# Two attention and mixer layers on one core: the second layer's channel mixers in groups of 3, 4, 3, 3, 3 tiles, a third buffer for VectorE's softmax blocks, and new ranks and instruction orders

## The chip, the cores and the metric

The kernel runs as one program on one core of a Trainium2 chip. The metric is the device time of one execution in microseconds. Before the change it is 1023.24 us, the median of three runs (1022.93 to 1025.7).

## The reference, cut to what matters

A sequence of 2048 rows of 448 numbers goes through attention, mixer, attention, mixer, with the same weights in both rounds:

```python
def _A_ref(x, wqkv, wo):                      # 16 heads of 28
    q, k, v = ...                             # from x @ wqkv
    scores = jnp.einsum("bhqd,bhkd->bhqk", q, k) * (Dh ** -0.5)
    p = _softmax(scores, axis=-1)
    o = jnp.einsum("bhqk,bhkd->bhqd", p, v)
    return ... @ wo
def _B_ref(x, w1, w2, w3, w4):
    h = _gelu(_layernorm(x) @ w1)
    hs = shifted_by_rows(h) @ w2              # four column groups, shifted by 1, -1, 2, -2 rows
    x1 = x + hs
    return x1 + _gelu(_layernorm(x1) @ w3) @ w4
x = x + _A_ref(_layernorm(x), A_wqkv, A_wo)
x = x + _B_ref(_layernorm(x), B_w1, B_w2, B_w3, B_w4)
# and both once more
```

Scores are 2048 x 2048 for each of 16 heads and two rounds; each of them needs an exponential.

## The kernel before, in words

**Tiles.** The rows are 16 tiles of 128. Attention works on blocks: 128 keys by 512 queries (or twice 128 by 256) of one head, one bank of the matmul accumulator (PSUM). There are 2048 blocks. Four heads form a head group, and a segment is one chunk of queries (`CHUNKS`: 4, 4, 4, 2, 2 tiles) with one head group and a run of key tiles (`ORDER`).

**Who takes the exponential.** `t_scores` lets TensorE write scores (line 1650) into banks 0 to 2 and banks 3 and 4 in turn; each such set is a *unit* of three or of two blocks, and `t_exp` lets ScalarE take the exponential of a whole unit in one instruction (line 1888), into PT, which has 15 places, six units deep. ScalarE takes each unit in order and is reserved for this from the first to the last. Some blocks go to VectorE instead, either from bank 6 or 7 or from bank 2 of a unit, which then has only two blocks for ScalarE (a *ring* block). Such a block is five VectorE instructions: `d_first` (line 1732) scales the scores out of PSUM into an integer buffer y, and `d_chain` (lines 1759, 1761, 1763 and 1766) makes 2 to that power with a cubic polynomial in a float buffer `fb` and adds the exponent. Before, y is `yd[0]` or `yd[1]`; `fb` has three buffers (`FB`), used also by the tanh form of GELU (`tanh_gelu`, lines 2152 to 2155) and by the softmax division (line 1995 and the transfer before it). For short times at the beginning and in the second layer, spare places of `vaug` serve too. A block is given to VectorE only if a y and a PD buffer are free at that moment in the plan, if VectorE's planned load is under `DTH` or `DDTH`, and if the rates `R_RATE` (ring) and `D_RATE` (the others) for that stretch allow it.

**PV and the division.** `t_pv` (line 1046) sums probabilities times V in bank 5, `t_norm` copies the sum out (lines 1969, 1971), spills it if the segment is not the last of its row, or divides by the row sums; `t_outproj` then applies wo.

**The mixer.** `t_mixA` multiplies by w1 (chunk by chunk), `t_mixB` does w2, w3 and GELU for a group of tiles from `BGROUPS`, and `t_w4` the last product. A group's w3 product comes in 14 parts of 128 features; a part of a group of n tiles is 128 n columns wide, and two parts share one bank when n is 2. While exponentials are still to come, VectorE copies each part out of PSUM (line 2313) and ScalarE takes one GELU over all 14 (line 2335), with a table load before it and one before the next exponential. After the last exponential (the plan's event "tail") ScalarE takes the GELU of each part straight from PSUM (line 2309). The groups before are tiles 0-2, 3-6, 7-10, 11-12 and 13-15 in both layers. `TANHW` marks one group of layer one that takes its GELU with tanh.

**What sets the order.** A planner (`Sched`) runs all these tasks in a simulated time with assumed costs. The dictionary `RANK` gives each task its priority; `Q_LEAD`, `K_FIRST`, `W_POS` and others say when loads and projections start. While TensorE would rest, the planner inserts fillers, four small matmuls on the identity matrix (lines 588 and 2381). The list of operations is then edited: `MOVES` puts single operations behind others of their engine, and `WEAVE`, a string with one letter for each operation (t TensorE, s ScalarE, v VectorE, g GpSimd, d the transfer queue), gives the order in which the engines' lists are merged. `rearranged` refuses an order in which an operation would read other data. Within an engine the instructions run in the order written.

Of the kernel before, what the change touches and what calls it, by code (L numbers as in the profile page):

```python
# [68 lines left out]
    "ttttvgssvvttttttttvvvvvvtvvvtvtstgtstsvtttvvtvvtvvtsttvvtsvvtttstvttstvttvvtgtsvtttvvstvttsvttvtttsvtttvttsttv",  # L69
    "svtgvgvvtttstvtttttvtttstvttvttvtdttttsvtvttvttsvttvtdttvtttvttvdstttttvstttttdvtstvtdtttttvtttttstvdttttvvstt",  # L70
    "vtsvttttttvvtvgtdtgttsvvtttttttvtsvtgttgvtttttsvttdttgttvttdttsvtdttvttdtvtdstvtdvttttsvtgtttttttvtstttttgttts",
    "vttttdvstttvtgsvtttvtttttttvtdsvttdtttdtsttvttdtgtsttvttttttstvttttttgtvtstvtdtttstvttttttttgttsttttttsttvtvtg",
    "tsttvttvtttvstvttvttttvttstttvtsvdtttdtvtvdvvsdvtvtttdttttvtsdvttvtdttdtvtsvtvdtttvtvtsttttvtttvttttstttttttts",
    "vtttvtttvstdttttvtgtttstvttttttsvtttttvstttvtttvttttsttvttttttsvtvttvtvtvvtsttvtvststtvdtttttgtttdvtstttttttvs",
    "tttttttttdtgsvtttttttsvgttttdtgdvsttdtvtgstvttttttttttsttttttsttvtttgtsttvttttttstvttgttttvstttvttdtsdttvttttt",
    "ttvsttttvtttsttvttvtvtvvtvstttvvsvtvttvtttttttvsttttvttsttvtttvttstvttdttdvsttttttttvtgttsttttstttttttttttsttt",
    "vtttvstgttvddsvtdtvttvdttttsvttttvtvttvvvsvtttvtvvsvtvttvtvttvttvttvsttttvttsvttgttttvtdtsdvttttdvsttvtttttttt",
    "tvttsvttdvttvvtvtdvsvttvdttvtttttdttttvsttsttvsttttttvttsttttvttvtttsvttttvtttsttttttvttttttttvtsttttvtttstvtt",
    "vttttttttvtsttttvtttvsttttvdtvsttttttvttttsttvttttttgtsttttttvtsttvtttvttdttttvstttttvtttsvtttdtvtttdtsvtttttt",
    "tttvtttstttvttvtttttsvtttttvsttttttvttttttttvsttvtttttvsgtttdtttvsttttvttttttsttvtttttvtgstttttvtstvttttttttvt",  # L80
# [691 lines left out]
RLO = 5  # L772
RHI = 7
RPRIO = 1
DWIN = 2
DTH = 0.4
XSHUT = (8, 83)
DLO = 6
DHI = 13
DPK = 2  # L780
DDTH = 1.3
# [6 lines left out]
TANHW = {(0, 0): 0, (0, 3): 0, (0, 7): 0, (0, 11): 1, (0, 13): 0, (1, 0): 0, (1, 3): 0, (1, 7): 0, (1, 11): 0, (1, 13): 0}  # L788
Sched.AGED = 0
Sched.TARGET = 0.695  # L790
Sched.LOW = 0
Sched.WIN = 1.582
Sched.LWIN = 3.6
GSL = 0
# [1691 lines left out]
```

## Time and profile before

| what | value |
|---|---|
| median of three runs | 1023.24 us |
| the profiled execution's own time | 1025.44 us |
| its span, first to last instruction | 1023.6 us |
| the first exponential of a unit starts at | 15.15 us |
| ScalarE's first table load for the GELU of the tail at | 969.87 us |
| operations in the plan (TensorE, ScalarE, VectorE, GpSimd, queue) | 7914, 880, 1572, 458, 362 |
| of them units of exponentials, blocks on VectorE, fillers | 782, 110, 837 |

An operation of the plan on TensorE is up to four matmuls; the profile counts them one by one. 110 blocks on VectorE appear in the profile as 109 in `yd` and one in `vaug`. Three stages follow from the table: a start of 15 us, a stage of exponentials of 955 us, and a tail of 54 us.

In profile rows, "x" is a count, "busy" the union of the group's time, "mean ns" the mean duration of one. An arrow "<-" names the output and its input, or, after a duration of idleness, what ended it.

### The profile page before, as it was taken

The numbers are of one execution on the slowest core, as the hardware profiler recorded it, in microseconds if no ns is written. First come the engines' busy times: TensorE is split into PE (matmuls) and PEld (weight loads), VectorE is DVE, ScalarE is ACT, GpSimd is POOL, SyncE is SP. The second block draws the span as 40 slices with busy tenths as digits, with TensorE's granted clock in tenths as the row PEclk, the third lists the DMA queues.
The fourth block names the chain that finished last, engine by engine and source line by source line (L and its number), as shares of the span: only waits on it lengthen the run. The fifth ranks groups of instructions, "written<-read, shape, count | busy, mean of one in ns | idle before, by whom it ended". The sixth has DMA issues, their size and how long they took to land.

```text
span 1023.6 us, 35818 instructions
## 1 busy us (share of the span) xinstructions
PE 968.4 (95%) x16107; PEld 408.1 (40%) x16109; DVE 814.0 (80%) x1572; ACT 981.7 (96%) x894; POOL 293.5 (29%) x462
## 2 busy tenths in 40 slices
PE   8999999999999999999999999999999999999998
PEld 4332443443333254343433443443433433444565
DVE  8777999989888958876877868698798589866651
ACT  8999999999999999999999999999999999999942
POOL 3312021531453016252325112012624120532230
PEclk9999999999999999999999999999999999999999
DMA  4634412320321014022231114423302020121101
GB/s 126 161 103 128 116 45 79 53 39 23 76 61 28 12 37 97 22 48 33 52 106 38 33 55 149 139 65 101 64 25 38 17 68 13 34 56 32 26 12 34
DMA packets 99393, 62.55 MB, mean 61 GB/s; under 512 B 68712, under 2 KB 88552, under 8 KB 99240
## 3 DMA queue, kind: packets, MB, share of 16 engines
q1 hardware_dynamic: 99240, 60.27, 23.2%
q8 instruction: 126, 2.06, 0.9%
q14 instruction: 27, 0.22, 0.1%
HBM read 28.16 MB, written 16.76 MB: 44 GB/s over the span
## 4 chain that ended last, share of the span: by engine, by line
ACT 70%; PE 24%; DVE 3%; DMA 1%; issue 1%; SPq 0%; DVEq 0%
ACT PT L1888 64%; PE ps L1055 14%; PE ps L1650 5%; PE ps L1046 4%; ACT h2T L2335 2%; PE ps L2381 1%; ACT fb L2154 1%; ACT L1888 1%; ACT hT L2136 0%; DMA rT<-ub 0%; DVE h2T L2313 0%; ACT L2335 0%; DMA obf<-in_A_x_dram 0%; DMA rscr<-rT 0%; DVE PD L1766 0%
## 5 line engine op out<-in xcount | busy, mean ns | idle before, releaser
L1888 ACT ACTIVATE PT<-ps 128x1024 bf16<-128x1024 f32 (+1 forms) x782 | 887.2, 1328 | 3.7 <-PE ps L1650 2.9
L1650 PE MATMUL ps<-qT,kT 32*128 32x512 bf16 (+1 forms) x2304 | 269.9, 335 | 24.1 <-ACT PT L1888 18.1
L1046 PE MATMUL ps<-PT,vaug 128*32 128x512 bf16 (+1 forms) x2420 | 246.2, 341 | 0.7 <-ACT PT L1888 0.2
L1055 PE MATMUL ps<-xT,w 128*32 128x512 bf16 (+4 forms) x2656 | 178.1, 344 | 5.0 <-DVE h2T L2313 3.4
L1650 PEld LDWEIGHTS ps<-qT,kT 32*128 32x128 bf16 x2304 | 69.7, 91 | 256.0 <-ACT PT L1888 224.7
L2381 PE MATMUL ps<-ident 128*32 128x256 bf16 x3348 | 145.1, 276 | 2.4 <-POOL ident L1140 1.5
L1046 PEld LDWEIGHTS ps<-PT,vaug 128*32 128x32 bf16 x2420 | 74.1, 95 | 89.4 <-issue 71.0
L2381 PEld LDWEIGHTS ps<-ident 128*32 128x32 bf16 x3348 | 94.3, 97 | 28.9 <-issue 11.8
L1995 POOL TENSOR_TENSOR otn<-ub,fb 128x512 bf16<-128x512 f32 (+1 forms) x31 | 35.8, 1154 | 212.8 <-DMA fb<-rscr 212.8
L1732 DVE TENSOR_SCALAR yd<-ps 128x512 int32<-128x512 f32 x109 | 74.5, 685 | 22.8 <-PE ps L1650 21.4
L1055 PEld LDWEIGHTS ps<-xT,w 128*32 128x32 bf16 (+1 forms) x2656 | 69.5, 95 | 56.8 <-issue 23.3
L1761 DVE SCALAR_TENSOR_TENSOR fb<-fb,yd 128x512 f32<-128x512 f32 x109 | 79.7, 734 | 0.7
L1055 PE MATMUL ps<-w,h2T 128*32 128x448 bf16 x1120 | 75.4, 355 | 4.4 <-ACT h2T L2335 4.3
L1759 DVE SCALAR_TENSOR_TENSOR fb<-yd 128x512 f32<-128x512 uint16 x109 | 78.3, 722 | 0.8
L1766 DVE SCALAR_TENSOR_TENSOR PD<-yd,PD 128x512 int16<-128x512 int16 x109 | 75.9, 698 | 1.6
L2313 DVE CAST h2T<-ps 128x512 bf16<-128x512 f32 (+1 forms) x70 | 44.4, 634 | 16.0 <-PE ps L1055 14.9
L1388 POOL TENSOR_TENSOR sq<-qT 128x512 bf16<-128x512 bf16 x24 | 28.5, 1190 | 96.1 <-DVE qT L1447 93.3
L1388 POOL TENSOR_TENSOR sq<-kT 128x512 bf16<-128x512 bf16 (+2 forms) x32 | 30.4, 950 | 83.1 <-DVE kT L1402 80.0
L1763 DVE TENSOR_SCALAR PD<-fb 128x512 bf16<-128x512 f32 x109 | 50.9, 468 | 1.0
L1055 PE MATMUL ps<-xT,wk_pad 128*32 128x512 bf16 (+2 forms) x576 | 47.6, 359 | 0.8 <-DVE kT L1402 0.3
L1055 PE MATMUL ps<-xT,wq_pad 128*32 128x512 bf16 x512 | 43.2, 382 | 0.5 <-issue 0.5
L1650 PE MATMUL ps<-wk_pad,kT 32*128 32x512 bf16 x256 | 39.6, 384 | 4.3 <-ACT PT L1888 3.8
(189 smaller groups left out, 1195.4 us busy)
## 6 DMA issues: line engine op xcount, KB each, us to landing
uscr<-ub SPq DMA_DIRECT2D x28, 256.0 KB
ub<-uscr SPq DMA_DIRECT2D x28, 256.0 KB, 7.0
fb<-rscr SPq DMA_DIRECT2D x24, 256.0 KB
xnd<-xn SPq DMA_DIRECT2D x28, 128.0 KB, 2.3
xd<-x_res SPq DMA_DIRECT2D x16, 224.0 KB, 2.1
x_res<-xd SPq DMA_DIRECT2D x16, 224.0 KB, 4.5
w<-in_B_w_dram SPq DMA_DIRECT2D x5, 448.0 KB, 5.4
obf<-in_A_x_dram SPq DMA_DIRECT2D x16, 112.0 KB
```

The source lines that it names most:

```text
L1046: return lambda e: e.matmul(out=out, lhsT=lhsT, rhs=rhs, start=start, stop=stop, **kw)
L1055: r.append(e.matmul(out=out[c:c + w, :], lhsT=lhsT[:, c:c + w], rhs=rhs, start=start, stop=stop, tile_position=(0, c)))
L1388: return both("sq", 0.15 + NW * 0.0018, 0.07 + NW * 0.00104, lambda e: e.tensor_tensor(out=sq[:, si, 0:NW], in0=src, in1=src, op=ALU.mult) ...
L1650: yield op("pe", (0.005 + NW * 0.00042) / nc_, lambda e, i=i, kc=kc, j=j, g=g, qt=qt, a=a, NW=NW, bank=bank: e.matmul(out=ps[:, bank, i * ...
L1732: yield op("dve", c_ps(512), lambda e: e.tensor_scalar(out=y, in0=ps[:, bi(bank), :], scalar1=SCALE * L2E * FS, scalar2=-126.0 * FS, op0=A ...
L1759: yield op(D_[0][0], D_[0][1], lambda e: e.scalar_tensor_tensor(out=q, in0=lo, scalar=E2 / E3 * FS, in1=lo, op0=ALU.add, op1=ALU.mult), re ...
L1761: yield op(D_[1][0], D_[1][1], lambda e: e.scalar_tensor_tensor(out=q, in0=q, scalar=E1 / E3 * FS * FS, in1=lo, op0=ALU.add, op1=ALU.mult) ...
L1763: yield op(D_[2][0], D_[2][1], lambda e: e.tensor_scalar(out=pdt, in0=q, scalar1=E3 / FS ** 3, scalar2=E0, op0=ALU.mult, op1=ALU.add), rea ...
L1766: yield op(D_[3][0], D_[3][1], lambda e: e.scalar_tensor_tensor(out=pdt.bitcast(I16), in0=hi, scalar=128.0, in1=pdt.bitcast(I16), op0=ALU. ...
L1888: yield op("act", 0.069 + n * w * 0.000833, lambda e, bk=bk, s0=s0, n=n, w=w: e.activation(out=PT[:, s0:s0 + n, 0:w], in_=ps[:, bk[0]:bk[0 ...
L2313: ev = op("dve", c_ps(m * NW), lambda e, hr=hr, pv=pv: e.tensor_copy(out=hr, in_=pv), reads=[("ps", bi(b))], writes=hk, touch=[b])
L2381: return [e.matmul(out=ps[32 * c:32 * c + 32, bi(b), 0:256].rearrange("p (a n) -> p a n", n=128), lhsT=ident[:, 32 * c:32 * c + 32], rhs=i ...
```

## The change

- Layer two's groups for w2 to w4 become tiles 0-2, 3-6, 7-9, 10-12 and 13-15 (`BGROUPS`; `TANHW`'s key follows).
- `Y_SHARE = 1`: the first of the three `fb` buffers may also serve as y, seen as integers.
- All ranks, rates, leads and thresholds get new values, most of them near the old ones.
- `MOVES` and `WEAVE` are new throughout.

```diff
-BGROUPS = {0: ..., 1: [[[0, 1, 2]], [[3, 4, 5, 6]], [[7, 8, 9, 10]], [[11, 12]], [[13, 14, 15]]]}
+BGROUPS = {0: ..., 1: [[[0, 1, 2]], [[3, 4, 5, 6]], [[7, 8, 9]], [[10, 11, 12]], [[13, 14, 15]]]}
-DPRIO = 3.5
+DPRIO = 3.293
-DWIN = 2
+DWIN = 2.589
-XSHUT = (8, 83)
+XSHUT = (11, 80)
-DDTH = 1.3
+DDTH = 1.294
-UPRIO = 2
+UPRIO = 1.933
-Sched.TARGET = 0.695
-Sched.LOW = 0
-Sched.WIN = 1.582
+Sched.TARGET = 0.697
+Sched.LOW = 0.066
+Sched.WIN = 1.653
-W_POS = (6, 9, 17, 5, 5, 5, 25, 21)
-V_FIRST = 1.366
-K_FIRST = (0.756, 0.932, 1.363)
-Q_FIRST = (0.531, 1.956, 2.405)
+W_POS = (8, 12, 19, 4, 5, 6, 23, 15)
+V_FIRST = 1.35
+K_FIRST = (0.399, 0.692, 1.096)
+Q_FIRST = (0.247, 1.622, 2.423)
+Y_SHARE = 1
...
             if r[1] == "v":
                 v, k = vbuf(r)
                 return v.bitcast(I32), k
+            if r[0] == "f":
+                return fb[:, num1(r), :].bitcast(I32), [("fb", num1(r))]
             return yd[:, num1(r), :], [("yd", num1(r))]
...
-        YS = ["y0", "y1"]
+        YS = ["y0", "y1"] + FB[:Y_SHARE]
```

`R_RATE`, `D_RATE`, `RANK`, `Q_LEAD`, `MOVES` and `WEAVE` are replaced as wholes. The letters of the two `WEAVE` strings can be counted:

| letter | engine | before | after |
|---|---|---|---|
| t | TensorE | 7914 | 7883 |
| s | ScalarE | 880 | 883 |
| v | VectorE | 1572 | 1605 |
| g | GpSimd | 458 | 455 |
| d | transfer queue | 362 | 362 |
| all | | 11186 | 11188 |

Up to the last GELU over 14 parts inside the stage of exponentials (the one of tiles 3-6 of layer two), both strings hold 784 letters s; both show it by a run of over fifty t behind it. Behind it stand 95 letters s before and 98 after. Up to it the strings hold 1422 and 1447 letters v, and 404 and 401 letters g. Toward the end of both strings stand fourteen s with mostly four t between them, and behind the last s come 76 letters t before and 82 after, with eight d each.

More of the change, by code (lines that the diff above doesn't have):

```diff
@@ L73 @@
[L73 to L77, printed above, removed]
@@ L168 @@
[L168 to L169 removed]
+    "ttttvgssvvttttttttvvvvvvtvvvtvtstgtstsvtttvvtvvtvvtsttvvtsvvtttstvttstvttvvtgtsvtttvvstvttsvttvtttsvtttvtstttt",
+    "vvsggvtttvttstttttvttsvttttvtvttdtttsvttvtvttsvttvtdttvtstttvtvdtttttsvttttdtttsvttvdtttvtttttvtstdtvtttstvtts",
+    "tvttvtttttvvdtttstvtvvgtttgtttstvvtttttvvttgtgsvttdttttttttsvttgtvtdttvtdstvtdttvtdvtsttvtgtttttvtstttttgtttsv",
@@ new lines @@
+    "ttttvstttvtgsvtttvtttttttvtsvttttvtdstdvttdttdgtstdttvttttdtstttvttttttvgtstttvttdstvtttttttttgtstttttsvttttvt",
+    "gstvtttvtvvtsttvtttttvtvtttvsttttvdsdtttvdvtttttvtdvtsdttvttdtttvsdvtttvtttvtstvtttvttsttvtvtvttvttttsttttttsv",
+    "tttvtttvsttttvtgttttstvttttttsvtttttvsttvttttvttttsttvtttsvttvtvtvtvttstttvttvststtvdvtttttdtttvttdsttdtvtgtts",
+    "ttttttttttsvtdttttttdsvgttttdtdvsttttvtttgtstvttttttsttttttsttvtttgtsttvttttttsvtttttvtttsttvttgtstvdttdtvtttt",
+    "ttvsttttttvtstttvtvsttvtsvttvtvttvttvtttvtvtvstvttttsvttvtttsvdttttdtttttgtsttttttvgtsttttgtstvtttttgttttttstt",
@@ new lines @@
+    "vtttvsttvddsvttdvttvvdttvttsvtvtdvttvtttvttstvttvttvvsvtvttvtttvtttvsvttttvttsvtttgtttvtdtsdvtttttdtttvtttsttv",
+    "ttttttvsvtttvtvvtvtvsvttvttvttttttttsvttsttvsttttttvttsttvtttttvtsvttttttvtstttvtttttvttttvtstttvttttsvttttttt",
+    "tvttttstvtttttvtstttvttvdstttvtttttttsvttttttvgttttstttttvtstvttttvtttttvtdstttvtdttvtsttvttttvtttsttvtttttttt",
+    "tvstttvtttvtdtttsvtttttvsvttttttttvtttttsvttttttvtstvtttvdtsvttttttttttsgttttttttttgsttttttvsttvtttvttdttstttt",
+    "ttstvtttdttvtttttdttsvtdtttvtdttsvttdtttvtdttttvstttttvttttttstttvttttvttstvtgtttvsdttttvtttgttttsttttvttttsvt",
@@ new lines @@
+    "tttvttttsvttttttvtsttvtttttvtttttstttvtttvsttvttttvttdtttttvstdtttttvtsttttdttvttttttvtstttttttttsvtttvdtvsttt",
+    "ttvttsttvtttttttttgttstttttttvgstttvttdttvsttttvttttttvstttvtttttvttdsttttdvtvsdttttvdttttttttvtstttttvttstttt",
+    "ttvtttvsttttvttttstvtttttvgstttttttttvtstttvttttvsvttttvdsttvtttvttstttttvttttttsdvttttvvtttsvtdttvttttstvttdt",
+    "ttvtttvsvttttgvsgttvtdtgtttttgtvttttstvttttvttvvtgstgtvdttgtvtdttgtsvtttttgttvtttdsttgtttvtttgttvsdtgttvtttgsv",
+    "tttdtgttvtttgttvtsttttgtttgtvsttgttttgttvtsgttvtdttttttgtsvtttttgttvtttgdsvttttgttgsttttttvttttsvtttttstvttttt",
@@ new lines @@
+    "tvgtsttdtvtttstttvtttttttvttsttvttttstvtttttvtvtdsttvtttsttvsvstvtdtvtttdtttgsttttttttstvttttttvtttttvtsttttvt",
+    "ttsttttstvttttttttvtttsttgtttsttvttttttstvtttvtttsvtttttvtsttttvttttvtttvtsttttvtsvtttttvtttvvgggsttvttgtttsvv",
+    "tttgvtdtttvgttsttttdttsvtttttvtttttgdstttttttsvttttgttttvtttttstvtttttvtdsttvtgvsvttttvtdttttttsttvttttvttvtts",
+    "ttvtttvtstttvtttvtttttvstdttttvttsttvtvtttsvttttttvtttsttvttttvtttvtsttttvttsvtttvgttttttttsttttttvsvtttvttttv",
+    "sttttvdtttsvttttvttttttsvtttttttvttttsttvtttdttttsvttttvttstvtdtvttttttvtsttttvttttsvtttvtttvstttvttvttsttvttt",
@@ new lines @@
+    "tttvtttsvtttttttvttgstttttttvtstttvttttttvvdtvttttttvttttvtdtttvttttvtvdtttvtstvtttvtvgttgvtttvtvgtstgtvtvvttg",
+    "ttdvgsgtttgttttttvsgtttvtttgvtdtsgvtgttttgvtstdgtvtvtgttvttttsgtvdttttgvstttgtvdttttgvtstgtvttttttgtsttvtttttg",
+    "tvgtgstgtdtgvtttsvtttvgttvtstgtvttgtvttdttstvtttvttsvttttdttgtttttstdttttdtdvttsdtvttttvdsttstvtsttvtttttttttv",
+    "sttvtttvsdtttvtttvgstttttvsgtvttttvgtsgtttttvttttstgtvttttvgtsttttttstttttvsttttttvtvgdsttvttttttttsvtttttvtdv",
+    "stttvsvttttsttttvtttvtsvtttttttvtsttvttvsttvtttvtsttvtttttvttvtgstgtvttvtgsgvttdttvtttstvtttvttsttttvttttvtdtt",
@@ new lines @@
+    "stttvtttsvtttdvttttttttvsttvttdtvtsttvtgtttttttvsttttvttgttstvttvtvttsgdvtttvgsttttvttstgttvttttttstvttttgtttt",
+    "tttstvtgttttstgtvgttttsvttttvttsvtdgtttttvtttttsttttvttttvstttvtvttttgtvsttttgttttvttstttvttttvtdttvsttttvttst",
+    "vtttgttttttttstttttvtttsvttttvdttsttvttttttvstttttvttvtdtsttvtttvtsttvtdtttttvttsttttvtttsvtttvtttvsttttvtttts",
+    "tvttttttvttvsttttgvtsttttttttvtttsttvttttsvtttvtttvsttttvttttstvtttttttvsvtttttvsttvtttttvttttstvtttttsttvttvt",
+    "tsvttttvtttstvtttttttttvsvtttttttvtttsttvttttvttttstvttttttttvstttttvdttvstttttttttttttvtttttttsttvtttttvtttdt",
@@ new lines @@
+    "tstttvtttttvstttvttdttttttttttttsvttttttttttttvtstttttttvtttttttvtttstvtttttttttvtsttttttttvtttttttvttttvtttvv",
+    "ttttvttttvdtttvttttvttvdttttvtttvsvtttvtttvtttvvtgttgvtvvtsgtttttgttttgttvtttsttgttvtttttttttstvtttvttttdvtstg",
+    "dtvgttttvtttttttttgsvtdgtttgttttvtttvtttttstgvttttgtdvgttstgtgtttttttgtdgvtsgtdttttgttttttttttvtttgstgttttvttt",
+    "ttttstgtvttttgttvtsgtdvtttttttgdvsttdvttttttdttttttttttvtgsttvtttgttttttvttsttttttttttgttttttttttvtstdvttttttv",
+    "dtsttdgttttdtttttttttvttsttttvtttttttttsvttttvtvtdsvttttgttttttvttttstttttvttttttdtttgttgvdsttttttttvtstvtdtts",
@@ L170 @@
+    "ttttsttststtttttttttvtttsvttttvstttvtsttvtvtgstgtvtvtstgtgtvtsvttgtvttgttttttvtttgvttttdvtttvtttttttttttttvtvt",
+    "tvtttvttttdttttttttttttttttttsttsttsttttsttttsttttsttttsttttsttttsttttsttttsttttsttttsttttsttttttttttttttvtttt",
+    "dttttttttttvttttdtttttttttvttttvdtttdttttttttttvttttdttttttttttvttttdttttttvdd",
 )
```

168 lines of the change are left out of this document (66 added, 102 removed), and 99 rows, old and new, of the table MOVES.

## Prediction

> **What bounds the kernel now.** I read the page's busy shares, then its chain of work, then the engines' busy time by stages.
>
> ```profile
> span 1023.6 us, 35818 instructions
> ...
> PE 968.4 (95%) x16107; PEld 408.1 (40%) x16109; DVE 814.0 (80%) x1572; ACT 981.7 (96%) x894; POOL 293.5 (29%) x462
> ...
> ACT 70%; PE 24%; DVE 3%; DMA 1%; issue 1%; SPq 0%; DVEq 0%
> ```
>
> ScalarE (ACT) and TensorE (PE) look equally full, but PE's figure contains fillers. The stages decide it. The view by windows has, after each engine's busy time, the number of instructions, and at the end the granted clock; the first row is from the first exponential to the last, the second the tail.
>
> ```profile
> core 0: us, PE busy (x) PEld busy (x) DVE busy (x) ACT busy (x) POOL busy (x), PEclk, DMA share, GB/s
> 15.15:969.87 954.72, 905.04 (x14710) 368.88 (x14710) 783.10 (x1482) 949.58 (x846) 279.95 (x424) 1.00 0.24 61
> 969.87:1023.60 53.73, 50.86 (x1170) 32.10 (x1159) 19.41 (x39) 20.16 (x33) 8.21 (x20) 1.00 0.07 22
> ```
>
> In the first stage ScalarE rests 954.72 - 949.58 = 5.14 us: that stage is as long as ScalarE's work. In the tail ScalarE is busy 20 of 54 us and TensorE 51: the tail is as long as TensorE's work. VectorE (DVE) rests 171.6 us in the first stage. So the time falls if ScalarE gets fewer blocks, or if the tail gets less matrix work; it rises if ScalarE is made to wait.
>
> ScalarE's price of a block comes from its groups, kept apart by shape, and from one piece of the chain in order of time (start, us, what), a pair of units of three and two blocks:
>
> ```profile
> L1888 ACT ACTIVATE PT<-ps 128x1536 bf16<-128x1536 f32 x375 | 580.8, 1549 | 2.9 <-PE ps L1650 2.3
> L1888 ACT ACTIVATE PT<-ps 128x1024 bf16<-128x1024 f32 x406 | 451.1, 1125 | 0.8 <-PE ps L1650 0.6
> 947.24 2.25 ACT PT L1888 x2
> ```
>
> One block more costs 1549 - 1125 = 424 ns. A pair takes 2.25 us, less than the sum of the two means because neighbours overlap; 2.25 - 5 x 0.424 = 0.13, so 0.065 us for each unit beside its blocks. With one last unit of a single block, ScalarE has 375 x 3 + 406 x 2 + 1 = 1938 blocks in 782 units, VectorE 110.
>
> **The change part by part.**
>
> *Blocks to VectorE.* The dictionaries of rates cannot be priced, but the letters of the order strings can. VectorE gets 33 operations more, GpSimd 3 fewer. GpSimd's three can only have gone to VectorE (a few operations have both engines as choices), which leaves 30. Copies out of PSUM for the regrouped GELU (below) might add one or two; I take none. A block is five operations: **six blocks more on VectorE**, four or five of them ahead of layer two's GELU of tiles 3-6 (25 more letters v up to it). ScalarE's letters agree: at that GELU both strings have the same number. Behind it, before has 1 + 62 + 32: a GELU, 58 units with 4 tanhs, and the tail's 32. After has 98, and the tail needs more (next point), some 38, which leaves 55 units. Three units fewer are seven or eight blocks; with one or two ring blocks fewer, six. Gain: 6 x 0.424 + 3 x 0.065 = **2.7 us**; with five blocks and two units, 2.25.
>
> *What it costs VectorE.* The five operations of a block are, on the page:
>
> ```profile
> L1732 DVE TENSOR_SCALAR yd<-ps 128x512 int32<-128x512 f32 x109 | 74.5, 685 | 22.8 <-PE ps L1650 21.4
> L1761 DVE SCALAR_TENSOR_TENSOR fb<-fb,yd 128x512 f32<-128x512 f32 x109 | 79.7, 734 | 0.7
> L1759 DVE SCALAR_TENSOR_TENSOR fb<-yd 128x512 f32<-128x512 uint16 x109 | 78.3, 722 | 0.8
> L1766 DVE SCALAR_TENSOR_TENSOR PD<-yd,PD 128x512 int16<-128x512 int16 x109 | 75.9, 698 | 1.6
> L1763 DVE TENSOR_SCALAR PD<-fb 128x512 bf16<-128x512 f32 x109 | 50.9, 468 | 1.0
> ```
>
> Their means add to 3.31 us; six blocks are 19.8 us, three moved operations at most 2.2 at 0.73 each. VectorE's 171.6 us of rest hide that, so nothing is charged. The page's slices of 25.6 us (tenths busy) show where that cover is thin, and the timeline of ScalarE and its list of waits (total us, times, longest) what it costs when it is gone: PSUM copies or a tanh's operand come late and ScalarE waits.
>
> ```profile
> DVE  8777999989888958876877868698798589866651
> ...
> 753.30 0.63 ACT L2154 ACTIVATE fb<-fb 112x512 f32<-112x512 f32 x1 [1.09 <-DVE fb L2153]
> ...
> 865.77 20.45 ACT L1888 ACTIVATE PT<-ps 128x1536 bf16<-128x1536 f32 x18 [0.70 <-PE ps L1650]
> 887.30 5.97 ACT L1888 ACTIVATE PT<-ps 128x1536 bf16<-128x1536 f32 x5 [1.08 <-PE ps L1650]
> ...
> ACT PT L1888 <- PE ps L1650: 2.9, 5, 1.1
> ACT fb L2154 <- DVE fb L2153: 1.1, 1, 1.1
> ```
>
> One such wait is at most 1.1 us. [...]
>
> ```profile
> L1761 DVE SCALAR_TENSOR_TENSOR fb<-fb,yd x109: 616/684/1766, 91.0 to 965.4; 128x512 f32<-128x512 f32 x109
> ```
>
> The same shape takes 616 to 1766 ns. [...]
>
> *The third y buffer.* It adds no instruction. It lets a third block leave its PSUM bank while two chains are under way, and takes an `fb` from the other chains, the tanhs and the division for about one chain, 3.3 us less the 0.69 of its first operation plus queueing. PT's six units hold six times 1.12 us (half a pair) = 6.7 us of exponentials, so one delay of 3 us in the division stays hidden. Charged at nothing; bounds below.
>
> *Groups 3 and 3 for 4 and 2.* ScalarE's timeline shows where the tail begins, and that the GELU over the first nine parts of tiles 7-10 already falls into it; so no table load is saved or added. Below it the tail's matrix work by shape.
>
> ```profile
> 969.87 1.28 ACT L2309 ACT_TABLE_LOAD   x1
> ...
> 987.45 3.18 ACT L2335 ACTIVATE vaug<-vaug 128x3584 bf16<-128x3584 bf16 x1
> 990.53 1.05 ACT L2335 ACTIVATE kT<-kT 128x1024 bf16<-128x1024 bf16 x1
> ```
>
> ```profile
> L1055 PE MATMUL ps<-xT,w 128*32 128x384 bf16 x224 | 9.3, 326 | 0.0
> ...
> L1055 PE MATMUL ps<-xT,w 128*32 128x256 bf16 x228 | 7.8, 273 | 0.0
> ...
> L1055 PE MATMUL ps<-xT,w 128*32 128x512 bf16 x72 | 4.6, 380 | 0.0
> ...
> L1055 PE MATMUL ps<-xT,w 128*16 128x256 bf16 x16 | 1.9, 273 | 0.0
> ```
>
> Four matmuls are one operation: 384 columns 9.3 / 56 = 0.166 us, 256 columns 7.8 / 57 = 0.137, 512 columns 4.6 / 18 = 0.256. Of the 228, 48 belong to w1 of the last tiles (16 operations of 112 outputs: three matmuls of 32 and one of 16, the last row), so w3 of the tiles 7-12 costs 45 x 0.137 + 4.6 = 10.8 us of this tail. After the last unit, before has 325 letters t; after has 304 to 318, by whether I put the last unit one letter s earlier or later. Everything but that w3 product is the same there: 126 operations with w4 (nine tiles), 56 with w3 of 13-15, 77 others, 259. That leaves 45 to 59 of 0.166 us, 7.5 to 9.8 us: the tail would be 1.0 to 3.3 us shorter. With the last unit where six blocks put it, the count is 318; I take **1.0 us**. The loss bound: one more part of four operations, 0.66 us, for each that slips out of the first stage; five of them, as before for tiles 7-10, are 3.3.
>
> *Ranks, edits, fillers.* The start's letters are the same up to the first exponentials: nothing. The new order can take away ScalarE's 5.14 us of rest at best; at worst, by the nearest rows, it doubles it. I take nothing. 31 letters t fewer are fillers, priced at nothing: they run where TensorE would rest, and the granted clock is 1.00 in both stages. If the clock fell for want of them, the tail would pay; no row shows such a fall.
>
> The sum: -2.7 - 1.0 = -3.7 us. On the profiled execution (1025.44 us, of which 1023.6 are span) that is 1021.7; this execution lies 2.2 us over the median of 1023.24, so the forecast for the median is **1019.5 us**.
>
> **The rivals.**
> - *Slower: VectorE becomes late for ScalarE.* Place: 100 to 205 us, where VectorE's digits are 9, and 740 to 890 us, where the waits above stand. Price 1.1 us for each wait. Four waits eat the gain of 3.7; one for each of six chains gives 6.6 - 3.7 = +2.9, 1026; a second for each through the lent `fb`, 13.2 - 3.7 = +9.5, 1033. For it: the digits, and an `fb` lent in the middle of tanhs. Against: 110 blocks now go with waits of 4.0 us together, 0.04 us a block.
> - *About the same: the gain is given back in small waits*, ScalarE's rest growing by 1 to 3 us as the new order meets late copies, and the tail unchanged: 1021.5 to 1022.5.
> - *The change does not do what it says:* the 33 operations are other work, ScalarE keeps 1938 blocks, and only the tail's 1.0 us remains: 1022.2.
> - *More than forecast:* the tail gives its 3.3 us and ScalarE's rest halves (2.6): 1023.24 - 2.7 - 3.3 - 2.6 = 1014.6; with half of each extra, about 1017.
>
> **How the numbers follow.** A measurement of this kernel tells about 0.3% (3.07 us) from no change, so "faster" begins below 1020.17. The forecast has a chance of 0.53, within 1018 to 1021, two thirds of it below the bound; more than forecast 0.17; small waits 0.12; not what it says 0.06; slower 0.12. Faster: 0.53 x 0.68 + 0.17 + 0.02 for a lucky tail = 0.55; of the slower case, which begins at the bound of 1026.3, 0.10 lies beyond; the rest, 0.35, is within. The range goes from half of the extra gain, 1016, to the small waits and a part of the slower case, 1023.8.
>
> **What would show it.** Right: about 116 blocks at line 1732, some of them in `fb`; 1932 blocks in 779 units; ScalarE's rest in the first stage near 5 us; its first table load of the tail near 967 us; twice 56 operations of 384 columns more and none of 256 with w3 of layer two's tiles 11-12; a tail of about 53 us. Wrong: ScalarE resting more than some 8 us in its first stage, 110 blocks as before, or a tail over 55 us.

## The result, and the profile after

The changed kernel takes **1028.05 us** (median of nine runs, 1025.95 to 1030.65), the kernel before on the same chip 1024.47 us. The ratio is 1.0036, 95% interval 1.0021 to 1.0052: slower by 0.36%, where 1019.5 us and a gain were forecast. A second measurement of the same pair on another chip (among the experiments) gave 1026.12 against 1024.47, ratio 1.0015, interval 1.0004 to 1.0026. The size of the loss therefore varies; its sign does not.

The page of the changed kernel's profiled execution (1026.93 us) begins with the span and the busy times, and has the shares of its chain:

```profile
span 1025.2 us, 35604 instructions
...
PE 964.0 (94%) x15982; PEld 406.5 (40%) x15985; DVE 828.3 (81%) x1605; ACT 980.4 (96%) x897; POOL 289.1 (28%) x459
...
ACT 73%; PE 19%; DVE 6%; DMA 1%; issue 1%; SPq 0%; DVEq 0%
```

The chain still runs through ScalarE for nearly three quarters; TensorE's share fell from 24 to 19%, VectorE's rose from 3 to 6%.

The view by windows, with the stage of exponentials and the tail as for the kernel before (PE, PEld, DVE, ACT and POOL busy, clock at the end):

```profile
15.08:969.10 954.02, 897.66 (x14565) 366.06 (x14566) 796.72 (x1514) 947.18 (x842) 274.83 (x421) 1.00 0.24 61
969.10:1025.20 56.10, 53.11 (x1186) 33.05 (x1179) 20.10 (x40) 21.29 (x40) 8.93 (x21) 1.00 0.09 26
```

ScalarE's work in the stage fell by 949.58 - 947.18 = 2.40 us (forecast 2.7). But the stage is only 0.70 us shorter, because ScalarE's rest grew from 5.14 to 6.84 us, and the tail grew by 2.37 us, from 53.73 to 56.10, where 1.0 us less was forecast. So the two profiled executions differ by 1.6 us of span; the medians differ by more, which the experiments explain.

The groups by shape show that the change does what it says:

```profile
L1898 ACT ACTIVATE PT<-ps 128x1536 bf16<-128x1536 f32 x377 | 583.9, 1549 | 6.0 <-PE ps L1658 3.4 <-PE ps L1054 1.8
L1898 ACT ACTIVATE PT<-ps 128x1024 bf16<-128x1024 f32 x400 | 446.6, 1124 | 0.5 <-PE ps L1658 0.3
...
L1742 DVE TENSOR_SCALAR yd<-ps 128x512 int32<-128x512 f32 x90 | 61.7, 685 | 22.2 <-PE ps L1658 21.6
...
L1742 DVE TENSOR_SCALAR fb<-ps 128x512 int32<-128x512 f32 x24 | 16.4, 684 | 2.5 <-PE ps L1658 2.3
```

377 x 3 + 400 x 2 + 1 = 1932 blocks are left to ScalarE, in 778 units; 90 + 24 blocks start in `yd` and `fb`, two more in spare places, 116 in all. In the tail, the products with w3 and w1 by shape (x500 is 125 operations of four matmuls, 56 of them for tiles 13 to 15; x48 and x16 are w1):

```profile
L1063 PE MATMUL ps<-xT,w 128*32 128x384 bf16 x500 | 22.1, 326 | 0.0
...
L1063 PE MATMUL ps<-xT,w 128*32 128x256 bf16 x48 | 1.9, 273 | 0.0
L1063 PE MATMUL ps<-xT,w 128*16 128x256 bf16 x16 | 1.9, 272 | 0.0
```

125 - 56 = 69 operations of 384 columns belong to tiles 7 to 12, where 45 to 59 were forecast. 69 x 384 = 26496 columns against 45 x 256 + 18 x 512 = 20736 before: 5760 more, 56 x 128 = 7168 of which would be the whole of one tile. It is tile 10: it moved from the group 7-10, of whose 56 operations only 18 were left for the tail, to the group 10-12, all of whose 56 stand in it (the other 13 of the 69 are those of the group 7-9). That a group has to wait for its last tile is how the plan is made; no run tests it by itself.

One thing is new in the clock. Around the GELU of layer two's first paired group, the view by windows of 2 us has:

```profile
502.00:504.00 2.00, 1.00 (x40) 0.70 (x28) 2.00 (x5) 2.00 (x1) 1.75 (x6) 1.00 0.00 0
504.00:506.00 2.00, 1.75 (x20) 0.81 (x24) 1.93 (x6) 1.97 (x3) 2.00 (x6) 0.58 0.42 85
506.00:508.00 2.00, 2.00 (x28) 0.97 (x24) 0.69 (x2) 1.88 (x2) 1.92 (x4) 0.56 0.23 46
508.00:510.00 2.00, 2.00 (x38) 0.74 (x26) 1.14 (x2) 0.86 (x1) 0.35 (x1) 1.00 0.35 74
```

TensorE rests for 0.90 and 1.25 us between 500.7 and 504.3 us, the clock is then granted at half for 3.4 us, and the next scores come late: ScalarE is busy for 0.86 of the last 2.00 us. Such a window of 3.4 us lowers the mean clock of an execution of 1024 us by 0.0017, so the clock that is listed with each run tells how many it had: 1.000 none, 0.998 one, 0.997 two, 0.995 three. The nine runs of the changed kernel had 15 (1.67 for each run); the kernel before has 0.3 to 0.5 for each run, and its runs with one take 1.3 to 1.8 us longer than those with none (medians on four chips, 8 to 15 runs with one on each; on a fifth chip, with five such runs, 0.5 us).

### The profile page after: what moved, and what is told of

Read it like the earlier page. It is cut to its first block, busy times and chain, and to the rows that moved or that the text cites. A ratio compares the mean times of both kernels' runs of the same rounds, so it can differ in the third digit from the quotient of the medians.

```text
span 1025.2 us, 35604 instructions
## 1 busy us (share of the span) xinstructions
PE 964.0 (94%) x15982; PEld 406.5 (40%) x15985; DVE 828.3 (81%) x1605; ACT 980.4 (96%) x897; POOL 289.1 (28%) x459
## 4 chain that ended last, share of the span: by engine, by line
ACT 73%; PE 19%; DVE 6%; DMA 1%; issue 1%; SPq 0%; DVEq 0%
ACT PT L1898 67%; PE ps L1063 11%; PE ps L1658 4%; PE ps L1054 3%; ACT h2T L2345 2%; ACT fb L2164 1%; DVE PD L1776 1%; DVE st L1248 1%; PE ps L2391 1%; ACT L1898 1%; DMA uscr<-ub 0%; DVE h2T L2323 0%; ACT hT L2146 0%; DVE xn L1268 0%; DVE fb L1769 0%
## 5 line engine op out<-in xcount | busy, mean ns | idle before, releaser
L1063 PE MATMUL ps<-xT,w 128*32 128x384 bf16 (+4 forms) x2656 | 177.9, 344 | 5.7 <-DVE h2T L2323 2.1
L2391 PEld LDWEIGHTS ps<-ident 128*32 128x32 bf16 x3224 | 91.7, 97 | 30.8 <-issue 11.7
L1063 PE MATMUL ps<-w,h2T 128*32 128x448 bf16 x1176 | 78.3, 361 | 4.7 <-ACT h2T L2345 4.2
L1742 DVE TENSOR_SCALAR yd<-ps 128x512 int32<-128x512 f32 x90 | 61.7, 685 | 22.2 <-PE ps L1658 21.6
L1776 DVE SCALAR_TENSOR_TENSOR PD<-yd,PD 128x512 int16<-128x512 int16 x90 | 64.9, 722 | 1.1
L1771 DVE SCALAR_TENSOR_TENSOR fb<-fb,yd 128x512 f32<-128x512 f32 x90 | 64.0, 712 | 0.4
L1769 DVE SCALAR_TENSOR_TENSOR fb<-yd 128x512 f32<-128x512 uint16 x90 | 63.0, 704 | 0.2
L1054 PE MATMUL ps<-PD,vaug 128*32 128x512 bf16 (+1 forms) x145 | 43.4, 339 | 1.0 <-DVE PD L1776 1.0
L1063 PEld LDWEIGHTS ps<-w,h2T 128*32 128x32 bf16 x1176 | 31.9, 98 | 30.9 <-issue 10.6
```

The costliest lines, as they stand in the source:

```text
L1054: return lambda e: e.matmul(out=out, lhsT=lhsT, rhs=rhs, start=start, stop=stop, **kw)
L1063: r.append(e.matmul(out=out[c:c + w, :], lhsT=lhsT[:, c:c + w], rhs=rhs, start=start, stop=stop, tile_position=(0, c)))
L1742: yield op("dve", c_ps(512), lambda e: e.tensor_scalar(out=y, in0=ps[:, bi(bank), :], scalar1=SCALE * L2E * FS, scalar2=-126.0 * FS, op0=A ...
L1769: yield op(D_[0][0], D_[0][1], lambda e: e.scalar_tensor_tensor(out=q, in0=lo, scalar=E2 / E3 * FS, in1=lo, op0=ALU.add, op1=ALU.mult), re ...
L1771: yield op(D_[1][0], D_[1][1], lambda e: e.scalar_tensor_tensor(out=q, in0=q, scalar=E1 / E3 * FS * FS, in1=lo, op0=ALU.add, op1=ALU.mult) ...
L1776: yield op(D_[3][0], D_[3][1], lambda e: e.scalar_tensor_tensor(out=pdt.bitcast(I16), in0=hi, scalar=128.0, in1=pdt.bitcast(I16), op0=ALU. ...
```

## The experiments

All ratios are to the kernel before, run on the same chip. The versions were measured on several chips, so differences between their medians that are told without a chip are across chips. "The changed kernel" is then its first measurement, 1028.05 us; its second, 1026.12, would make such a gain 1.9 us smaller. Where fillers are added or operations left out, this is done to the finished order, with one line behind the rearranging of the plan; positions are those of the order's list, and nothing else moves:

```diff
             P = P.rearranged(MOVES, "".join(WEAVE))
+            P = P.altered(DROP, MORE, SC.fill)   # leaves out DROP, puts fillers on the named banks behind positions
```

**First theory:** the loss is the tail plus windows of half clock that come because there are fewer fillers while TensorE waits for a GELU. **Rival:** VectorE is late for ScalarE, and the clock does not matter.

### More fillers, fewer fillers, less w3

```diff
 e1_fillers (changed kernel)        +MORE = {5592: ["b6"] * 9, 8837: ["b6"] * 5, 9820: ["b6"] * 16}
 e2_less_w3 (changed kernel)        +DROP = {the second of the four w3 operations of each of 14 features, tiles 10-12}
 e3_thin (kernel before)            +DROP = {3736 to 3749, 9792 to 9807 without 9794}   # 14 and 15 fillers
 e4_more_fillers (kernel before)    +MORE = {2720: ["b6"] * 9, 3749: ["b6"] * 16, 9807: ["b6"] * 14}
```

> The changed kernel with 30 more fillers: nine behind the last filler at 503.0 us, sixteen behind that at 902.5 us, five behind that at 825.9 us; nothing else is changed. Theory (windows of half clock, about 1.45 us each, come where TensorE rests while it waits for a GELU): the mean clock of most runs rises to 1.000 and the median falls by about 2 us, from 1028.05 to about 1026. Rival (the whole loss sits in ScalarE's waits for VectorE and in the tail): clock and time stay as in the changed kernel, within 0.5 us. If other places lose the clock too, the fall is 0.5 to 1.5 us.

Measured: 1025.13 us, ratio 1.0004 (0.9995 to 1.0012); 2.9 us less than the changed kernel, 0.27 windows for each run. As the theory had it, and more than it had.

> The changed kernel, leaving out 14 of the 56 w3 operations of tiles 10 to 12 in the tail (one of the four parts of the sum for each of 14 features), so that its matrix work there is 14 x 0.166 = 2.3 us less, as much as one tile's share is (56 operations of 128 columns, 3.0 us) to within a quarter. Theory (the tail is as long as TensorE's work): the tail falls from 56.1 to about 53.8 us and the time by 2.3 us, with the clock of the other parts unchanged. Rival (the tail waits for other engines): less than 1 us.

Measured: 1027.81 us, ratio 1.0032 (1.0020 to 1.0044). The tail fell from 56.10 to 54.83 us, 1.27 of the 2.04 us that TensorE's work fell. The whole time hardly fell: the profiled run had three windows, two of them at 795 us, and ScalarE waited 4.1 us there. Inconclusive for the time, but a first sign that a place near 795 us matters.

> The kernel before with 29 fillers taken out: 14 ahead of 366.2 us and 15 ahead of 899.9 us, so that TensorE rests 3.5 us instead of 1.9 ahead of w4 in both places; no other instruction is changed. Theory: each of these rests brings a window of 3.4 us of half clock in most runs; clock 0.997 and 2 to 3 us more. Rival (fillers do not matter for the time): no change of more than 0.5 us, whatever the clock does.

Measured: 1026.81 us, ratio 1.0024 (1.0014 to 1.0034), 2.3 us more, 0.993 to 0.998 of clock in its twelve runs. With rests of 3.49 and 3.28 us in its profile, where the kernel before has 1.96 and 1.82, no run kept the whole clock, and time went with it. The windows of its profile, for one of the two places (rest of TensorE, then w4, then the next scores):

```profile
898.30:901.60 3.30, 0.02 (x8) 0.01 (x4) 0.75 (x2) 3.30 (x2) 0.67 (x1) 1.00 0.13 45
901.60:905.00 3.40, 3.40 (x40) 1.48 (x44) 0.24 (x2) 3.37 (x3) 0.05 (x1) 0.50 0.00 0
```

ScalarE does not lose in the window itself (3.37 of 3.40 us busy); it waits for the scores behind it, 1.07 us here and 1.16 us at the other place.

> The kernel before with 39 more fillers: sixteen behind the last at 366.2 us, fourteen behind that at 899.9 us, nine behind that at 262.0 us. Theory: if some runs of the kernel before lose a window too, the clock becomes 1.000 in all and the median falls by 0.5 to 1 us, below 1024; if it never does, nothing changes (within 0.3 us). Rival: fillers delay w4 behind them, and the time rises by 0.1 to 1 us.

Measured: 1024.81 us, ratio 0.9998 (0.9990 to 1.0007). No window in eleven runs, and yet no gain, where 0.5 to 1 us was expected: its runs were 1.05 us longer than those runs of the kernel before that had no window either. In its profile some 0.6 us of this lie in the tail (54.4 us), in which nothing was added. Why is open.

> The kernel before with nine fillers more behind the last at 366.2 us and nothing else. Theory: this is the place where the kernel before loses its windows of half clock (0.4 to 0.5 for each run); they go, the clock is 1.000 in all runs and the median falls by 0.5 to 0.8 us. Rival (added fillers cost about as much as the windows, as the run with 39 of them suggests): no change within 0.3 us.

```diff
 f1_before_9_at_366 (kernel before)  +MORE = {3749: ["b6"] * 9}
```

Measured: 1024.28 us, ratio 1.0001 (0.9992 to 1.0010), one window in eleven runs. The windows go, the median does not fall as expected: 0.3 of a window for each run, some 0.5 us, was too little to see in an interval of this width.

> The changed kernel with the 30 more fillers of the first of these runs (503, 826 and 902 us), leaving out 14 of the 56 w3 operations of tiles 10 to 12 in the tail: the earlier run without them, at an undisturbed clock. Theory (the tail is as long as TensorE's work): tail 56.05 - 2.0 = 54 us, median 1023.1 against 1025.13 with the fillers alone. Rival (about half of it is lost to waits, as in the earlier run: 1.3 us of 2.0): 1023.9. If nothing is gained, the tail hangs on another engine.

```diff
 e5_fillers_less_w3 (changed kernel) +MORE as e1_fillers, +DROP as e2_less_w3
```

Measured: 1022.88 us, ratio 0.9986 (0.9976 to 0.9995); the tail 54.79 against 56.05 us. So at an undisturbed clock 2.04 us less of TensorE's work in the tail are worth 1.3 us of the tail, as the rival had it: the tail hangs on TensorE, though not for every tenth. The median is 2.25 us below that of e1, as the theory had it, but e1 ran on another chip, and both intervals are nearly 2 us wide.

### Groups or ranks?

The plans with the old and the new groups are the same up to the regrouping at 905 us. So the edits can be kept up to there, with the planner's own order behind it, and the two halves of the change exchanged one at a time. "Ranks" stands here for everything that is new but the groups: ranks, rates, thresholds, the third y buffer, and the edits up to that place.

```diff
 c1 (changed kernel)   MOVES: those below 9855; WEAVE: its first 9855 letters, then the planner's order
 c2  as c1             BGROUPS[1]: 7-10, 11-12
 d1 (kernel before)    MOVES: those below 9860; WEAVE: its first 9860 letters, then the planner's order
 d2  as d1             BGROUPS[1]: 7-9, 10-12
```

> The changed kernel with its edits of the order kept up to the regrouping (about 905 us) and the planner's own order behind it; groups 7-9 and 10-12. Its partner has groups 7-10 and 11-12 and is the same up to there. This one has 74 w3 operations of 384 columns for the tiles 7 to 12 in the tail (after has 70), so its tail should be 0.7 to 3 us longer than after's 56.1 us. Theory (the new groups make the tail longer): its tail is the longer of the two by 1 to 2.4 us. Rival (the new ranks make it longer, the groups shorten it): the shorter of the two by 1.2 us (by columns) to 3 us (by 0.177, 0.256 and 0.137 us for each operation).

> As the run above, with groups 7-10 and 11-12 in place of 7-9 and 10-12: new ranks and new edits up to 905 us, old groups. In the tail it has 33 w3 operations of 512 columns and 56 of 256. Theory (the groups make the tail longer): tail about 55 us, 1 to 2.4 us shorter than its partner's. Rival (the ranks do): 1.2 to 3 us longer than its partner's.

> The kernel before with its edits kept up to the same place (about 904 us) and the planner's own order behind it; groups 7-10 and 11-12. In the tail 18 w3 operations of 512 columns and 54 of 256 (before has 18 and 45): a tail of about 55 us. It is the partner of the next run.

> As the run above with groups 7-9 and 10-12: old ranks, old edits up to 904 us, new groups, 71 w3 operations of 384 columns in the tail. Theory (the groups make the tail longer): 0.6 us (by prices of operations) to 1.8 us (by columns) longer than its partner's. Rival (the groups shorten it by what was forecast): 1 us shorter. If the two pairs of runs disagree in sign, the worth of the groups depends on the ranks, and neither cause stands alone.

Measured: c1 1029.22 us (ratio 1.0036, 1.0021 to 1.0050), c2 1029.07 (1.0042, 1.0027 to 1.0056), d1 1025.72 (1.0005, 0.9994 to 1.0015), d2 1028.19 (1.0026, 1.0016 to 1.0037). The tails, in the order c1, c2, d1, d2, one row from each profile:

```profile
971.39:1027.90 56.51, 53.55 (x1190) 33.53 (x1183) 21.00 (x41) 21.65 (x40) 8.91 (x21) 1.00 0.09 26
```

```profile
970.12:1027.80 57.68, 54.72 (x1253) 34.80 (x1245) 21.28 (x43) 20.69 (x36) 8.65 (x22) 1.00 0.09 25
```

```profile
970.60:1024.80 54.20, 51.24 (x1170) 32.49 (x1159) 19.49 (x39) 20.76 (x33) 8.20 (x20) 0.99 0.07 22
```

```profile
969.45:1026.30 56.85, 53.33 (x1182) 34.91 (x1170) 21.24 (x42) 21.48 (x39) 8.19 (x21) 1.00 0.07 22
```

With the old ranks the new groups lengthen the tail by 2.65 us; with the new ranks they shorten it by 1.17 us. With the old groups the new ranks lengthen it by 3.48 us. Each tail is that of one profile. **Neither cause stands alone**: under either half of the change the tail is 56 to 58 us, and only old ranks with old groups give 54.

### Which fillers did it?

```diff
 f2_after_9_at_503 (changed kernel)   +MORE = {5592: ["b6"] * 9}
 f3_after_16_at_902 (changed kernel)  +MORE = {9820: ["b6"] * 16}
```

> The changed kernel with nine fillers more behind the last at 503.0 us only. Theory (the windows come at three places: 504, 795 and 907 us): about one window for each run goes, 0.6 to 0.9 are left, and the median falls by 1.2 to 1.8 us to 1026.5. If the windows came mainly at 907 us, the fall is under 0.7 us.

> The changed kernel with sixteen fillers more behind the last at 902.5 us only. Theory: the rest of 2.1 us stands between solid fillers and solid w4, and no profile so far shows a window there: under 0.4 of a window for each run goes, and the median falls by less than 0.7 us. If it is the main place: 1.2 to 1.8 us.

Measured: f2 **1023.82 us**, ratio 0.9988 (0.9979 to 0.9996), 0.27 windows for each run; f3 1026.45 us, ratio 1.0022 (1.0013 to 1.0031), 0.67 windows. Against the changed kernel's 1028.05 us the nine fillers at 503 us gave 4.2 us, twice what was expected of them, and f2 is below the kernel before. f3 is 1.6 us below the changed kernel by its first measurement, where under 0.7 was expected, and at its level by the second (ratio 1.0015). But the window count cannot carry 4.2 us: 1.4 windows at 1.3 to 1.8 us are 1.8 to 2.5 us.

```diff
 g1_after_again            the changed kernel, unchanged
 g2_after_9_at_503_again   as f2
 g4_after_none_at_503      +DROP = {eleven of 5578 to 5592}   # the fillers there
```

> The changed kernel once more, unchanged, on the same chip as the next two. Theory (windows and nothing else): 1026 to 1027, about 2.4 us above the variant with nine fillers, with 1 to 1.7 windows for each run. If the rest at 503 us costs something of its own, it is about 4 us above that variant again, and its runs at full clock too.

> The changed kernel with nine fillers more at 503 us, a second time. Expected: 1023.8 again (1023.3 to 1024.5), 0.2 to 0.4 of a window for each run, ratio to the kernel before 0.998 to 1.000.

> The changed kernel without the eleven fillers between 501.6 and 503.0 us, so that TensorE rests from 500.7 to 504.3 us. Theory (a long rest costs one window of half clock, 1.4 to 1.8 us): every run has a window there; against the unchanged kernel, which has it in most runs but not in all, 0.3 to 1 us more. Rival (that place is not what matters): no change.

Measured on one chip: g1 1026.12 us with 1.08 windows, g2 1023.25 us (ratio 0.9989, 0.9979 to 0.9999) with 0.42, g4 1027.74 us (ratio 1.0025, 1.0014 to 1.0035) with 2.2; it is 1.6 us above g1, where 0.3 to 1 was expected. g1 is 2.87 us above g2, of which windows explain about 1.0; and runs with one window took 1026.26 in g1, 1024.59 in g2. **So the first theory was not enough.**

### A late transfer at 795 us

Comparing where ScalarE waits in each profile gave the second theory. Near 795 us it waits for 1.82 (changed kernel), 1.66 (g1), 1.88 (f3), 1.95 (c2), 3.32 (c1) and 4.10 us (e2), but 0.91 (e1), 0.64 (e5) and under 0.25 us (f2, g2, g4) where fillers were added or taken at 503 us. In the changed kernel, the list of TensorE's waits and ScalarE's timeline there have:

```profile
PE ps L1063 <- DVE fb L1769: 1.5, 1, 1.5
```

```profile
796.61 3.71 ACT L1898 ACTIVATE PT<-ps 128x1536 bf16<-128x1536 f32 x3 [1.81 <-PE ps L1054]
```

The first row names VectorE, but the matmul reads `xT`, which five transposes from `xn` fill. In the seven profiles with a wait of 1.66 us or more (h2, below, is the seventh) it goes on 3.7 to 4.7 us after the fifth was started (790.46 to 794.69 us in this one), and in all seven 0.20 us after the last of the 16 landings of that fifth transpose, as the traces record them (794.49 us in this one); behind the end of the last VectorE instruction it is 0.01 to 0.41 us. So the transfer releases it. Their issues on the transfer queue (SPq), and the kinds of packets from 785 to 787 us:

```profile
783.90 4.67 SPq L1273 DMA_TRANSPOSE xT<-xn  x3
788.63 0.55 SPq L1993 DMA_DIRECT2D rT<-ub  x1
789.22 2.50 SPq L1273 DMA_TRANSPOSE xT<-xn  x2
```

```profile
q1 hardware_dynamic: 533, 0.13, 85.5%
q8 instruction: 1, 0.02, 2.9%
```

An issue takes 1.2 to 1.3 us, but one of the five takes 1.5 to 2.7 us, and in all thirteen profiles of versions that keep the changed kernel's order here (those of the list above, and h1 and h2 below), it is the one during which an instruction load (queue q8) starts. In the seven with the long wait (the changed kernel, g1, f3, c2, c1, e2 and h2) it is the first or second, so that the later ones are late. The landings show a second loss, about as large: the next load follows 7 to 8 us behind (at 792.45 us in this profile) and falls on the data of the fifth, whose last part lands 2.3 to 3.2 us after the end of its issue. In the six others the load falls on the fourth or fifth issue, the next one comes after the matmul, and the fifth lands 1.1 to 1.3 us after the end of its issue. From the first issue to the last landing of the fifth it is 8.5 to 9.4 us in the six and 10.3 to 11.4 in the seven, and ScalarE's wait grows with it; the three waits over 3 us (c1, e2, h2) have a window of half clock behind them.

Why would fillers move a load? The page of the changed kernel counts 125 loads on q8 beside 15982 matmuls and 15985 weight loads, that of the kernel before 126 beside 16107 and 16109: in both there are 255.7 matmuls and weight loads to one load. Fillers ahead of this place move TensorE's instructions: nine fillers are 72 (f2's stage has 14601 matmuls and 14602 weight loads, the changed kernel's 14565 and 14566). **Second theory:** the fillers at 503 us helped because they moved the load, not because they filled a rest.

```diff
 h1_after_9_elsewhere (changed kernel)    +MORE = one filler behind each of 7107, 7144, 7185, 7193, 7273, 7366, 7445, 7918, 8001
 h2_503_filled_not_moved (changed kernel) +MORE = {5592: ["b6"] * 9}
                                          +DROP = {7107, 7164, 7185, 7437, 7823, 7963, 7992, 8039, 8331}
```

> The changed kernel with nine fillers more, one each at nine places between 657 and 743 us where TensorE rests 0.23 to 0.47 us; 503 us is as in the changed kernel. TensorE's instruction stream at 785 us is moved by 72 instructions as with nine fillers at 503 us. Theory (the place of the instruction load decides over the wait at 794 us): the load falls on the fifth transpose (near 789 us in place of 782 to 785 us), ScalarE waits 0 to 0.9 us there in place of 1.7 and more; about one window of half clock for each run stays; 1024.4 to 1025, some 1.5 us below the unchanged kernel's 1026.12. Rival (503 us alone matters): 1026 as before, with a wait of 1.7 us or more.

> The changed kernel with nine fillers more at 503 us and nine fewer between 657 and 775 us, one from each of nine runs of six or seven, so that the stream at 785 us is not moved. Theory (two separate costs): windows at 503 us gone (0.3 to 0.5 for each run), the wait at 794 us back at 1 to 4 us; 1024.5 to 1025.5, 1.2 to 2 us above the variant with nine fillers at 503 us (1023.25). Rival (503 us alone matters): 1023.3 and no wait at 794 us.

Measured: h1 **1023.82 us**, ratio 0.9996 (0.9985 to 1.0007), 0.27 windows; h2 1026.86 us, ratio 1.0026 (1.0011 to 1.0042), 1.17 windows. Both went further than expected (h1 0.6 us below its range, h2 1.4 us above), because windows went and came with the wait. The second theory holds on both sides, and the rival (503 us alone) falls: with 503 us as it was, the loss is gone, and with 503 us filled it is back. The transfer queue of h1, with the packets from 787 to 789 us:

```profile
781.84 3.82 SPq L1286 DMA_TRANSPOSE xT<-xn  x3
785.71 0.55 SPq L2006 DMA_DIRECT2D rT<-ub  x1
786.31 3.38 SPq L1286 DMA_TRANSPOSE xT<-xn  x2
```

```profile
q1 hardware_dynamic: 721, 0.17, 42.1%
q8 instruction: 1, 0.02, 3.5%
```

The three transposes take 3.82 us and the two behind them 3.38: the load falls on the fifth. ScalarE waits 0.29 us. In h2 the load falls on the first:

```profile
783.58 5.29 SPq L1286 DMA_TRANSPOSE xT<-xn  x3
788.93 0.55 SPq L2006 DMA_DIRECT2D rT<-ub  x1
789.52 2.50 SPq L1286 DMA_TRANSPOSE xT<-xn  x2
```

```profile
793.00:795.00 2.00, 0.00 (x0) 0.00 (x0) 2.00 (x5) 1.42 (x2) 0.00 (x0) 0.94 0.36 12
795.00:797.00 2.00, 1.86 (x17) 0.66 (x17) 1.06 (x2) 0.00 (x0) 0.00 (x0) 0.50 0.08 19
797.00:799.00 2.00, 2.00 (x24) 0.51 (x19) 0.00 (x0) 0.55 (x1) 0.00 (x0) 0.70 0.25 97
```

In the first row TensorE rests; in the second its clock is halved, and ScalarE does nothing at all; in the third ScalarE works for 0.55 us. The late transfer can thus bring its own window: 4.03 us of waiting in one place. That fits the counts: versions in which the load is moved have 0.27 to 0.42 windows for each run (e1, e5, f2, g2, h1), and those in which it is not, 0.67 to 1.83 (the changed kernel, g1, c1, c2, e2, f3, h2). g4 stands apart, since it makes a window of its own at 504 us.

One rival is left: h2 loses time because it has nine fillers fewer between 657 and 775 us. Its trace speaks against that. Unit by unit, the profiled execution of h2 falls 4.5 us behind that of h1 between 790 and 810 us, 1.4 us at a second window at 907 us, and only 0.2 us between 657 and 780 us. The changed kernel's falls behind h1's by 2.1 us between 790 and 810 us and by 1.7 us at its window at 504 us.

What the moved load leaves is seen in the stage and tail of h1:

```profile
15.50:964.66 949.16, 896.51 (x14601) 366.16 (x14602) 795.77 (x1514) 946.92 (x841) 275.22 (x421) 1.00 0.25 61
964.66:1020.70 56.04, 53.12 (x1186) 33.02 (x1179) 20.12 (x40) 21.32 (x40) 8.94 (x21) 1.00 0.09 26
```

ScalarE rests 949.16 - 946.92 = 2.24 us, less than the 5.14 of the kernel before; the tail is as long as in the changed kernel.

### A version below both

> The changed kernel with the old groups 7-10 and 11-12, the ranks of layer two's later chunks set once more so that the plan has less w3 in the tail (18 w3 operations of 512 columns and 56 of 256), nine fillers more at 503 us, and the planner's own order from 551 us on. 115 blocks on VectorE. Theory (stage about 2.5 us shorter than before's, tail as before's, clock kept): 1022 to 1023, below both kernels; what it loses by the missing edits behind 551 us is not known, and if they are worth more than 2 us it ends above 1024.

Its edit is new values for the ranks of layer two's chunks 2 to 4, the old `BGROUPS`, the nine fillers, and `MOVES` and `WEAVE` cut off at 551 us, with the planner's own order behind. Measured: 1024.16 us, where 1022 to 1023 was expected, ratio 0.9995 (0.9985 to 1.0005), tail 54.98 us, 0.58 windows. No gain over f2 and g2. These two, the changed kernel with nine fillers at 503 us on two chips, are below both kernels with all the work done (e5 leaves a part out): 0.9988 and 0.9989, with intervals that end at 0.9996 and 0.9999, about 1.2 us.

## Why the prediction was wrong, point by point

- **Blocks to VectorE, 2.7 us: right, but for one unit.** 1932 blocks, 116 on VectorE, 778 units (779 forecast; the difference matters below); ScalarE's work in the stage fell by 2.40 us.
- **What it costs VectorE, nothing: right as far as shown.** The rival by which VectorE becomes late for ScalarE was the slower one, with places between 740 and 890 us. The loss did come there, and the list of waits names VectorE, but what was late was a transfer. With the load elsewhere (h1), ScalarE rests only 2.24 us with all 116 blocks on VectorE. Why one operation of a chain takes from 616 to 1766 ns (median 684, line 1761 before) no run shows.
- **The third y buffer, nothing:** not tried by itself. h1's 2.24 us of rest are an upper bound for what it costs there.
- **Groups 3 and 3 for 4 and 2, -1.0 us: wrong, +2.37 us.** The step that failed is the count of w3 operations, taken from the letters behind a last unit whose place was guessed: 59 where 69 stood. Four units went, not three, so the last unit stands one letter s earlier, where the string has 329 letters t behind it and not 318; the step's own 259 others then leave 70. Its price was low as well: 0.166 us for an operation of 384 columns, where the 125 of the tail took 22.1 / 125 = 0.177. Count and price together turn a w3 product of 9.3 + 10.8 us, forecast at 9.3 + 9.8, into 22.1. The loss bound of that step, +3.3 us, does hold the value; the forecast went with the wrong end. A question that the step did not ask is which tiles a group holds: in the plan a part of a group can only be made early if all its tiles are ready early, and tile 10 went from a group of which most was made early to one of which nothing was. The 2x2 shows that the tail depends on the ranks as much: -1.17 us for the groups with the new ranks, +2.65 with the old.
- **Ranks, edits, fillers, nothing: wrong.** The step took the granted clock of 1.00 in a mean over 955 us for a clock that never falls, though 3.4 us at half clock take only 0.002 from that mean; and one execution had none where others had one. "If the clock fell for want of them, the tail would pay" was wrong as well: the scores behind the window pay, 1.1 us in e3. Within this step lies a loss that the forecast put at nothing: the new order puts two instruction loads on the transposes of one chunk's queries. Its price, with the windows that come with it, is seen between h2 and h1, 1026.86 - 1023.82 = 3.0 us.
- **What would show it:** "a tail over 55 us" was named as the sign of a wrong forecast, and came.

The sum: the forecast change was -3.7 us, the measured one +3.6 in the first comparison and +1.65 in the second. The tail is 3.4 us of the error, 7.3 in the first comparison and 5.35 in the second. The rest, 2 to 4 us, is of the size of what the wait at 795 us and its windows cost (3.0 us); the windows at 504 and 902 us have a part in it that was not separated. Without that wait, the change is worth -2.4 us and the shorter rest in the stage against +2.3 us in the tail, and h1 with 0.9996 shows what remains: nothing that can be measured.

A window of half clock lasted 3.4 us in the profiles of the changed kernel, e3, g4 and h2, and the nine runs of the changed kernel had none, one, two or three. TensorE had not rested through all of the time ahead of it: in the 3.4 us ahead of the fall at 504.3 us it had rested 1.95 us, ahead of the one at 795 us in h2 2.0 us. And rest is not the whole of it: in two profiles the clock fell where TensorE had rested 0.39 us (c2, at 960 us) and not at all (s5, at 943 us), and in that of the changed kernel it stayed at 1.00 behind 2.08 us of rest ahead of 904.6 us. The kernel before has no window and no rest over 2.0 us in its profile, and yet 57 of its 152 runs beside the experiments lost some clock. So no rest from which the clock falls is shown.

What stays open: why an instruction load stretches the issue of a transpose and holds up its data; what besides rest halves the clock, and from which share; why e4, without any window, gained nothing; and how the windows divide among 504, 795, 902 and 960 us, of which each was seen in some profile.

## What to carry to other kernels

Look for the matrix work that is left when the longest engine ends: a group of tiles is as late as its last tile, and its whole product goes with it. Read the clock in windows of a few microseconds and over several runs, not as a mean: here it was halved for 3.4 us where TensorE had rested 1.95 and 2.0 us of the 3.4 before (and twice behind 0.39 us or none), and in e3 the scores behind the matmuls at half clock paid, with 1.07 and 1.16 us. And before a gain is put down to what was filled or removed, make a version that moves the instructions by the same number without it: here nine fillers spread between 657 and 743 us took away the loss as nine at 503 us did. Where a wait is put down to one engine, look up when the transfers that it reads have landed.

## What the runs showed of the hardware

- In the changed kernel 125 instruction loads (one packet of 0.02 MB each on queue q8) stand beside 31967 matmuls and weight loads of TensorE, 255.7 to one, and come 7.2 to 8.8 us apart from 760 to 792 us. Of five transposes in thirteen profiles, the one during whose issue a load started took 1.5 to 2.7 us to issue in place of 1.2 to 1.3. Long issues come without a load too: elsewhere in the changed kernel's profile nine of the 18 other issues of transposes over 1.45 us had no load on them, and eleven that a load overlapped took 1.19 to 1.44 us.
- Where a load fell on the data of the fifth transpose, its last part landed 2.3 to 3.2 us after the end of its issue, elsewhere 1.1 to 1.3 (seven profiles against six). 72 instructions of TensorE more ahead of the place moved the load from the second issue of five (the changed kernel) to the fifth (h1).
- A wait of 1.5 us that the profile of the changed kernel puts down to VectorE was that of a transfer: the matmul started 0.20 us behind the last landing of the fifth transpose in all seven profiles.
- With the same program, one execution has no window of half clock and the next has three: of the nine runs of the changed kernel the one without took 1025.95 us, the three with three 1030.26 to 1030.65.
